# A second mixture of experts: sums read from PSUM, operands in another order, raw pieces and stored operands moved

## The chip, the cores and the metric

The kernel runs on one core of a Trainium2 chip. The metric is device time in microseconds of one execution; before the change the median of three runs is 2117.43 us (2113.62 to 2118.29). Engine names are those of the profile: PE is TensorE's matmul, PEld its weight load, DVE VectorE, ACT ScalarE, POOL GpSimd, SP SyncE, which here only issues DMAs.

## The reference

Three layers run one after the other over 2304 tokens of width 512: retention attention, a first mixture, and the second mixture, which this change is about:

```python
def _moe2_ref(x, w_gate, w1, w2):          # N=2304, D=512, E=8 experts, F=1024
    logits = x @ w_gate
    P = np.exp(logits - logits.max())
    for _ in range(8):                      # row and column sums in turn
        P /= P.sum(1, keepdims=True) + 1e-09
        P /= P.sum(0, keepdims=True) + 1e-09
        P *= N / E
    out = 0
    for e in range(E):
        out += P[:, e:e+1] * (np.maximum(x @ w1[e], 0.0) @ w2[e])
```

All of it is fp32. The kernel keeps that precision on PE by splitting each operand into a high half (rounded to fp32r) and a low half (operand minus high half), and multiplying three pairs: high by high, high by low, low by high.

## The kernel before, in words

The second mixture cuts the hidden width into 32 units of 256 (8 experts x 4) and the tokens into 3 passes of 768, so there are 96 steps, `s` from 0 to 95; `q = s // 32` is the pass and `u = s % 32` the unit. Both matrix products of a unit are done as a 2 x 2 block scheme with seven products in place of eight: seven token operands (`X1K`, `T2`, ...) times seven weight operands of w1 (`AK`, `S2`, `S1`, `AL`, `S3`, `S4`, `BL`), each of six matmuls of 384 columns (`product`, L933). Their sums are formed with adds on DVE out of three kinds of PSUM bank, `x`, `y` and `z`: `p1` copies the first product, `u2`, `p5` and `u3` (L1118 to L1146) are partial sums in SBUF.

In pass 0 (L1069) a step also makes the operands that the later passes reload. `weight_tasks` (L618) is a list of small closures for the next unit: ACT rounds the high halves (`hi`), POOL subtracts (`lo`, L686, and the sums of w1 pieces, L662), and SP writes the finished parts to DRAM. `mixed_tasks` (L577) does the same for the four mixed operands of w2: four sums on DVE in one closure (L590), high halves on ACT (L596), low halves on POOL (L600), eight writes. The list is worked off by `slot(k)` and between the six `mm2` (L951), which multiply the activations of the step before by w2, plainly, and add into `acc` on DVE (L976, L985). Four PSUM banks `m` hold mm2's results, and PE stops when DVE has not emptied the oldest. The relu is split as well: ACT takes the high half (L943), DVE the low one (L947). The last product of a step (`BL`) and its relu are put off into the next step (`late_product`). In steps 0 to 4 the row and column sums of the gate run on DVE between products (`tick`). From step 4 on, `tasks` holds DVE and ACT work that forms the token operands of the next pass; five of these pieces (`late`) have to wait for the last step of a pass.

In passes 1 and 2 (L1312) a step has seven places `k`. Place k runs `first_(s, k)`, the k-th product of this step with its adds and the fold of relu and gate weight (L1171), then `after`, which splits activation operands for the second product (ACT high half L1182, POOL low half L1183, POOL differences L1186), and then `second_(s-1, k)`, one block of nine matmuls (L1268) of the step before, whose result DVE adds into `acc` (L1281), through two double banks `p`. Which operand the block of place k reads is in `ORDER_S`; the blocks E7, E5, E6 and E4 read differences of activations (D3, D1, D2, D4), E3 reads B22. Behind each use SP reloads that weight operand for the next step, 256 KB at a time. `finish` (L1288) forms a pass's output from the seven sums once the pass is over.

Every engine works in the order in which the program issues to it: a closure's place in a list is its place in the queue of each engine that it uses, SP's DMAs included. No scheduler moves anything (`manual_schedule`).

## Time and profile before

| | |
|---|---|
| runs | 2117.43 us median (2113.62 to 2118.29) |
| profiled execution | 2117.14 us, its span 2115.3 us |
| mean granted TensorE clock | 0.975 of full |
| busy | PE 1993.8 us (94%), DVE 1556.8 (74%), POOL 1441.1 (68%), ACT 675.8 (32%) |
| pass 0 | about 501 to 1111 us, passes 1 and 2 from there to the end |

The span runs from the first to the last instruction; the profiled execution's time has 1.8 us more around it. Busy time of PE is a modelled figure, since matmuls overlap, so a step is better judged by when the next one starts. Steps are cut where ACT copies the first product of a step: line L1106 in pass 0 (32 of them, from 501.3 to 1073.5 us) and L1196 in the later passes (64, from 1111.4 to 2081.5 us).

### The profile page before, as it was taken

How to read it: one execution, taken by the hardware profiler on the slowest of the kernel's cores; microseconds unless marked ns; L12 is line 12 of the kernel's file. 1: busy time of each engine (PE TensorE's matmuls, PEld its weight loads, DVE VectorE, ACT ScalarE, POOL GpSimd, SP SyncE). 2: the span in 40 equal slices, each digit the busy share in tenths (PEclk: the TensorE clock that was granted, in tenths of full speed). 3: DMA queues.
4: the chain of work that ended last, by engine and by line, in shares of the span. 5: the costliest groups of instructions: out<-in, count | busy, mean ns of one | idle time of the engine just before them, and what ended most of it. 6: DMA issues, size and time to landing. Idle time of an engine off the chain costs nothing.

```text
span 2115.3 us, 35267 instructions
## 1 busy us (share of the span) xinstructions
PE 1993.8 (94%) x12369; PEld 1818.9 (86%) x12369; DVE 1556.8 (74%) x2318; ACT 675.8 (32%) x1408; POOL 1441.1 (68%) x1393
## 2 busy tenths in 40 slices
PE   7899999999888998999959999999998999999998
PEld 6688888877777887888859999999997999999997
DVE  7865877535877787887855787877776777777777
ACT  3334223334344343333423322222223322222221
POOL 4654555534576677777736788887877878787875
PEclk9999999999999899999989999999999999999999
DMA  8411111014667777777768888788786888788873
GB/s 314 161 40 36 55 37 44 26 55 144 205 234 249 250 253 251 251 277 278 268 196 245 261 251 249 251 249 253 239 252 206 273 252 249 248 238 262 250 252 119
DMA packets 269584, 434.74 MB, mean 206 GB/s; under 512 B 25936, under 2 KB 119008, under 8 KB 269152
## 3 DMA queue, kind: packets, MB, share of 16 engines
q1 hardware_dynamic: 269264, 432.47, 63.3%
q8 instruction: 99, 1.62, 0.3%
q14 instruction: 77, 0.63, 0.1%
q10 hardware_dynamic: 144, 0.02, 0.0%
HBM read 310.15 MB, written 122.23 MB: 204 GB/s over the span
## 4 chain that ended last, share of the span: by engine, by line
POOL 24%; DVE 20%; PE 15%; issue 6%; ACT 4%; DMA 1%; SPq 1%; POOLq 0%; DVEq 0%; ACTq 0%
POOL wo L1183 11%; POOL u L1186 5%; PE ps_m L963 5%; DVE mix L590 4%; DVE u L1171 4%; PE ps_y L933 4%; PE ps_p L1268 3%; POOL p L1186 3%; POOL r L1186 2%; POOL p L1345 2%; DVE acc L1281 2%; PE ps_z L933 2%; PE ps_x L933 2%; DVE wo L947 1%; ACT wo L1182 1%
## 5 line engine op out<-in xcount | busy, mean ns | idle before, releaser
L1268 PE MATMUL ps_p<-wi,wo 128*128 128x256 f32 x3969 | 550.0, 283 | 15.7 <-ACT acc L1279 5.4
L1268 PEld LDWEIGHTS ps_p<-wi,wo 128*128 128x128 f32 x3969 | 522.5, 189 | 36.0 <-ACT p L1196 22.5
L1281 DVE TENSOR_TENSOR acc<-ps_p,acc 128x768 f32<-128x768 f32 x427 | 400.2, 950 | 99.9 <-PE ps_p L1268 92.1
L963 PE MATMUL ps_m<-wo,wo 128*128 128x512 f32 x1152 | 296.9, 413 | 67.4 <-DVE acc L985 58.8
L933 PE MATMUL ps_y<-xh,wi 128*128 128x384 f32 x1152 | 342.6, 342 | 1.0 <-DVE u L1201 1.0
L963 PEld LDWEIGHTS ps_m<-wo,wo 128*128 128x128 f32 x1152 | 224.6, 198 | 126.9 <-DVE acc L985 70.9
L1183 POOL TENSOR_TENSOR wo<-u,wo 128x384 fp32r<-128x384 f32 x191 | 195.0, 1021 | 163.0 <-ACT wo L1182 160.6
L1182 ACT ACTIVATE wo<-u 128x384 fp32r<-128x384 f32 x191 | 100.4, 526 | 490.7 <-POOL u L1186 286.8
L933 PE MATMUL ps_z<-xh,wi 128*128 128x384 f32 x768 | 231.9, 343 | 2.4 <-DVE u L1151 2.4
L933 PE MATMUL ps_x<-xh,wi 128*128 128x384 f32 x768 | 227.6, 337 | 0.0
L933 PEld LDWEIGHTS ps_y<-xh,wi 128*128 128x128 f32 x1152 | 218.7, 194 | 3.3 <-DVE u L1201 1.2
L442 POOL TENSOR_TENSOR gl<-sg,gh 128x512 fp32r<-128x512 f32 (+1 forms) x80 | 95.6, 1195 | 173.1 <-ACT gh L441 134.9
L933 PE MATMUL ps_y<-xl,wi 128*128 128x384 f32 x576 | 196.8, 342 | 0.0
L430 PE MATMUL ps<-xh,wi 128*128 128x512 f32 (+1 forms) x640 | 186.4, 370 | 0.0
L455 PE MATMUL ps<-gh,wo 128*128 128x512 f32 (+1 forms) x640 | 184.2, 368 | 0.3
L686 POOL TENSOR_TENSOR wi<-r,wi 128x512 fp32r<-128x512 f32 x64 | 71.0, 1109 | 147.3 <-ACT wi L679 129.4
L933 PEld LDWEIGHTS ps_z<-xh,wi 128*128 128x128 f32 x768 | 145.7, 193 | 6.6 <-DVE u L1151 6.5
L1183 POOL TENSOR_TENSOR wo<-p,wo 128x384 fp32r<-128x384 f32 x127 | 148.1, 1166 | 2.2 <-ACT wo L1182 1.9
L933 PEld LDWEIGHTS ps_x<-xh,wi 128*128 128x128 f32 x768 | 142.4, 189 | 0.0
L440 DVE TENSOR_TENSOR sg<-ps,sg 128x512 f32<-128x512 f32 (+1 forms) x80 | 51.0, 637 | 120.6 <-ACT sg L439 118.5
L430 PEld LDWEIGHTS ps<-xh,wi 128*128 128x128 f32 x640 | 116.4, 188 | 23.5 <-issue 3.4
L455 PEld LDWEIGHTS ps<-gh,wo 128*128 128x128 f32 x640 | 116.2, 189 | 20.9 <-POOL wo L166 1.1
(151 smaller groups left out, 3844.4 us busy)
## 6 DMA issues: line engine op xcount, KB each, us to landing
wi<-first SPq DMA_DIRECT2D x448, 256.0 KB, 3.3
wi<-second SPq DMA_DIRECT2D x441, 256.0 KB, 3.2
first<-wi SPq DMA_DIRECT2D x90, 512.0 KB, 2.7
r<-in_w_dram SPq DMA_DIRECT2D x65, 512.0 KB, 4.7
second<-wo SPq DMA_DIRECT2D x96, 256.0 KB, 2.2
second<-wi SPq DMA_DIRECT2D x128, 128.0 KB, 1.9
second<-mix SPq DMA_DIRECT2D x128, 128.0 KB, 1.9
aux<-in_vk_dram SPq DMA_DIRECT2D x16, 544.0 KB, 6.1
```

Of the source, the lines that this page charges most:

```text
L430: nc.tensor.matmul(out=t[:, 0:n], lhsT=a[:, d, fs], rhs=x[:, d, t0 : t0 + n], start=d == 0 and a is wh and x is xh, stop=d == KD - 1 and a ...
L442: nc.gpsimd.tensor_tensor(out=gl[:, f, 0:n], in0=gf[:, 0:n], in1=r32(gh[:, f, 0:n]), op=ALU.subtract)
L455: nc.tensor.matmul(out=po[d][:, 0:n], lhsT=a[:, f, ds_], rhs=x[:, f, 0:n], start=f == 0 and a is wh and x is gh, stop=f == KF - 1 and a is wl,
L590: nc.vector.tensor_tensor(out=out, in0=a, in1=b, op=op)
L933: nc.tensor.matmul(out=t[:, 0:N], lhsT=w[:, o, hw, c], rhs=xq(q, x, hx, c), start=begin and c == 0 and i == 0, stop=end and c == 1 and i == 2,
L963: nc.tensor.matmul(out=t, lhsT=x[:, is_], rhs=w[:, h, f], start=f == 0 and k == 0, stop=f == 1 and k == 2,)
L1171: nc.vector.scalar_tensor_tensor(out=to, in0=c, scalar=0.0, in1=pr_of(s)[:, t * N : (t + 1) * N], op0=ALU.max, op1=ALU.mult,)
L1182: nc.scalar.activation(out=h, in_=src, func=ACTF.Copy)
L1183: nc.gpsimd.tensor_tensor(out=l, in0=src, in1=r32(h), op=ALU.subtract)
L1186: nc.gpsimd.tensor_tensor(out=to, in0=a, in1=b, op=ALU.subtract)
L1268: nc.tensor.matmul(out=t[:, j * QF : (j + 1) * QF], lhsT=x[:, js], rhs=w[:, o, hw], start=k == 0, stop=k == 2,)
L1281: nc.vector.tensor_tensor(out=e, in0=t[:, 0 : 3 * QF], in1=e, op=ALU.add)
```

## The change

In pass 0 the four mixed sums become four closures with a fifth, `begin`, ahead of them, in which ACT copies the left half of the raw w2 piece into the `y` bank that the step does not use; three of the sums read it there. They are placed between the tasks of w1 and those of w2 and one after the other between the mm2. The second add for `u3` goes: `p5` is now `z + p1` on DVE, and the three finished sums are written into the PSUM banks `x`, `z` and `y` themselves, from where relu reads both halves. `y` is two fixed banks, `x` gets two and `m` three. The raw w2 piece is loaded by `load_next` one step ahead, behind POOL's last read of the one before; the mixed operands of unit 0 are made in step 0 and no longer in step 31. Token tasks run one per step behind the fourth mm2. The stored operands of w2 are laid out so that two share one DMA.

In passes 1 and 2 the order of the blocks is E1, E3, E7, E5, E6, E2, E4: B22 comes second, and D3, D1 and D2 one place later. `p5` is formed by DVE out of PSUM, no longer by ACT and POOL, and the sums stay in PSUM until the fold. Weights come in five DMAs for the first product and four for the second. `after` stands ahead of the block. `finish` is on DVE alone and hands out one sum per step (two in the second step of a pass), and the late token tasks one per place.

```diff
     def mixed_tasks(s, raw):
-        def sums():
-            r = raw().rearrange("p b (j d) -> p b j d", j=2)
-            t = box["t"] = raw2[1].tile([P, 2, 2, QF], F32, tag="mix", name="mix")
-            for out, a, b, op in (
-                (t[:, 1, 1], r[:, 0, 1], r[:, 1, 1], ALU.add),
-                (t[:, 0, 1], r[:, 0, 0], r[:, 0, 1], ALU.subtract),
-                (t[:, 0, 0], t[:, 1, 1], r[:, 0, 0], ALU.subtract),
-                (t[:, 1, 0], r[:, 1, 0], t[:, 0, 0], ALU.subtract),
-            ):
+        def begin():
+            box["p"] = ys[(s + 1) % 2].rearrange("p (b d) -> p b d", b=2)
+            box["t"] = raw2[1].tile([P, 2, 2, QF], F32, tag="mix", name="mix")
+            nc.scalar.activation(out=box["p"], in_=raw()[:, :, 0:QF], func=ACTF.Copy)
+
+        def sums(i):
+            def go():
+                r = raw().rearrange("p b (j d) -> p b j d", j=2)
+                p, t = box["p"], box["t"]
+                out, a, b, op = (
+                    (t[:, 1, 0], p[:, 0], r[:, 0, 1], ALU.subtract),
+                    (t[:, 1, 1], r[:, 0, 1], r[:, 1, 1], ALU.add),
+                    (t[:, 0, 0], t[:, 1, 1], p[:, 0], ALU.subtract),
+                    (t[:, 0, 1], p[:, 1], t[:, 0, 0], ALU.subtract),
+                )[i]
                 nc.vector.tensor_tensor(out=out, in0=a, in1=b, op=op)
 
...
             def put():
-                for b in range(2):
-                    o = ((E6, E3), (E7, E5))[j][b]
-                    nc.sync.dma_start(out=w2st(s)[:, o, 0], in_=r32(w[:, b]))
-                    nc.sync.dma_start(out=w2st(s)[:, o, 1], in_=box["t"][:, b, j])
-
-            return [go, low, put]
-
-        return [sums] + high(1) + high(0)
+                d = part(second_store[s], (3, 1)[j], 2)
+                nc.sync.dma_start(out=d[:, 0], in_=r32(w))
+                nc.sync.dma_start(out=d[:, 1], in_=box["t"][:, j])
+
+            return [high, low, put]
+
+        return [begin] + [sums(i) for i in range(4)], rest(1) + rest(0)
 
+    def load_next(s):
+        e, u = divmod(s, NQ)
+        ahead2[s] = raw2[0].tile([P, 2, DM], F32, tag="r2", name="r2")
+        src = w2[e, u * QF : (u + 1) * QF, :].rearrange("(f p) d -> p f d", p=P)
+        nc.sync.dma_start(out=ahead2[s], in_=src)
...
-        second_ = [hi("w"), lo("w", slice(0, 1)), mixed[0], lo("w", slice(1, 2))]
-        second_ += [lambda: keep_plain(s - 1)] + mixed[1:]
+
+        def following():
+            if s < NU:
+                load_next(s)
+
+        mix = mixed[0]
+        second_ = [hi("w"), lo("w", slice(0, 1)), lo("w", slice(1, 2))]
+        second_ += [lambda: keep_plain(s - 1), following] + mixed[1]
         if s == NU:
-            return [load] + second_
-        ts = [load, sums(S1), hi("a"), sums(S3), hi("b"), hi(S1), lo("a", al), put(AK, 2)]
-        ts += [lo(S1, al), put(S1, 2), sums(S2), sums(S4), hi(S2), lo("b", al), put(BL, 1)]
-        return ts + [lo(S2, al), put(S2, 2)] + second_
+            return [load, mix[0]] + second_[:1] + mix[1:] + second_[1:]
+        ts = [load, sums(S1), hi("a"), mix[0], sums(S3), hi("b"), hi(S1), lo("a", al)]
+        ts += [put(AK, 2), lo(S1, al), put(S1, 2), sums(S2), sums(S4), hi(S2), lo("b", al)]
+        ts += [put(BL, 1), lo(S2, al), put(S2, 2), mix[1], second_[0], mix[2], second_[1]]
+        ts += [second_[2], mix[3], second_[3], mix[4]]
+        return ts + second_[4:]
...
+    for s in range(2):
+        keep_first(s, 0, 7)
...
-    psum = {tag: open_banks(tag, n) for tag, n in (("x", 1), ("y", 2), ("z", 1), ("m", 4))}
+    ys = []
+    psum = {tag: open_banks(tag, n) for tag, n in (("y", 2), ("z", 1), ("x", 2), ("m", 3))}
...
-    ORDER_S = ((E1, B11), (E7, D3), (E5, D1), (E6, D2), (E3, B22), (E2, B21), (E4, D4))
+    ORDER_S = ((E1, B11), (E3, B22), (E7, D3), (E5, D1), (E6, D2), (E2, B21), (E4, D4))
...
-        wt = weight_tasks(s + 1) if s else []
+        wt = weight_tasks(s + 1) if s else begun[2]
         if s == 0:
-            keep_first(0, 0, 7)
-        if s == 1:
-            keep_first(1, 0, 7)
-            keep_plain(0)
-        if s == NU - 1:
-            box = {}
-
-            def again():
-                box["r"] = raw2[0].tile([P, 2, DM], F32, tag="r2", name="r2")
-                nc.sync.dma_start(
-                    out=box["r"], in_=w2[0, 0:QF, :].rearrange("(f p) d -> p f d", p=P)
-                )
-
-            wt += [again] + mixed_tasks(0, lambda: box["r"])
+            load_first(2)
...
-            if tasks and k % 6 == 2 and s % 2:
-                tasks.pop(0)()
-            if xt and k >= 1:
-                xt.pop(0)()
+            if s == NU - 1 and k in (2, 5, 9):
+                drop_late()
...
-            for o in ORDER_F:
-                load_first_ops(NU, o)
+            for o, n in ((AK, 2), (S2, 2), (S1, 2), (BL, 1)):
+                load_first_ops(NU, o, n)
...
-        y = bank2("y")
+        y = ys[s % 2]
...
-        nc.scalar.activation(out=p5, in_=z[:, 0:N], func=ACTF.Copy)
+        nc.vector.tensor_tensor(out=p5, in0=z[:, 0:N], in1=p1, op=ALU.add)
...
-        for i in (3, 4, 5, 0, 1, 2) if s else ():
-            while i != 3 and len(wt) > 5:
+        for n, i in enumerate((3, 4, 5, 0, 1, 2) if s else ()):
+            mm2(s - 1, i)
+            for _ in range(-(-len(wt) // (6 - n))):
                 wt.pop(0)()
-            mm2(s - 1, i)
-            if wt:
-                wt.pop(0)()
+            if tasks and n == 3:
+                tasks.pop(0)()
             tick()
...
-        u3 = tmp("u3")
-        nc.vector.tensor_tensor(out=u3, in0=y[:, 0:N], in1=p1, op=ALU.add)
-        nc.vector.tensor_tensor(out=u3, in0=u3, in1=p5, op=ALU.add)
-        relu_high(s, 1, 1, u3)
-        relu_low(s, 1, 1, u3)
+        c = x[:, 0:N]
+        nc.vector.tensor_tensor(out=c, in0=y[:, 0:N], in1=p5, op=ALU.add)
+        relu_high(s, 1, 1, c)
+        relu_low(s, 1, 1, c)
         product(s, z, S4, X2L, False, True)
         tick()
-        nc.vector.tensor_tensor(out=u2, in0=z[:, 0:N], in1=u2, op=ALU.add)
-        relu_high(s, 0, 1, u2)
-        relu_low(s, 0, 1, u2)
-        while xt:
-            xt.pop(0)()
+        c = z[:, 0:N]
+        nc.vector.tensor_tensor(out=c, in0=c, in1=u2, op=ALU.add)
+        relu_high(s, 0, 1, c)
+        relu_low(s, 0, 1, c)
 
         def rest(s=s, y=y, p1=p1):
             product(s, y, BL, T4, False, True)
             tick()
-            nc.vector.tensor_tensor(out=p1, in0=y[:, 0:N], in1=p1, op=ALU.add)
-            relu_high(s, 1, 0, p1)
-            relu_low(s, 1, 0, p1)
+            c = y[:, 0:N]
+            nc.vector.tensor_tensor(out=c, in0=c, in1=p1, op=ALU.add)
+            relu_high(s, 1, 0, c)
+            relu_low(s, 1, 0, c)
...
+            load_first_ops(s + 1, S2, 1)
...
-            nc.scalar.activation(out=d["p5"], in_=d["z"][:, 0:N], func=ACTF.Copy)
+            nc.vector.tensor_tensor(out=d["p5"], in0=d["z"][:, 0:N], in1=d["p1"], op=ALU.add)
...
+            load_first_ops(s + 1, AK, 2)
...
         if k == 4:
             product(s, d["y"], S3, T3, False, False)
+            load_first_ops(s + 1, S1, 2)
+            c = d["x"][:, 0:N]
+            nc.vector.tensor_tensor(out=c, in0=d["y"][:, 0:N], in1=d["p5"], op=ALU.add)
             d["u3"] = tmp("u3")
-            nc.vector.tensor_tensor(out=d["u3"], in0=d["y"][:, 0:N], in1=d["p5"], op=ALU.add)
-            folded(s, d["u3"], 1, d["u3"])
+            folded(s, c, 1, d["u3"])
         if k == 5:
             product(s, d["z"], S4, X2L, False, True)
-            nc.vector.tensor_tensor(out=d["u2"], in0=d["z"][:, 0:N], in1=d["u2"], op=ALU.add)
-            folded(s, d["u2"], 1, d["u2"])
+            load_first_ops(s + 1, S4, 1)
+            c = d["z"][:, 0:N]
+            nc.vector.tensor_tensor(out=c, in0=c, in1=d["u2"], op=ALU.add)
+            folded(s, c, 1, d["u2"])
...
-            nc.vector.tensor_tensor(out=d["p1"], in0=d["y"][:, 0:N], in1=d["p1"], op=ALU.add)
-            folded(s, d["p1"], 0, d["p1"])
-        load_first_ops(s + 1, ORDER_F[k])
+            load_first_ops(s + 1, BL, 1)
+            c = d["y"][:, 0:N]
+            nc.vector.tensor_tensor(out=c, in0=c, in1=d["p1"], op=ALU.add)
+            folded(s, c, 0, d["p1"])
...
+        if i in (0, 3, 4, 6):
+            load_second_ops(s + 1, lead, n)
...
-            op(g, E2, E1, E2, ALU.add, (0, 0)),
...
-        fin = finish(q - 1) if u == 1 and q > 1 else []
+        if u == 1 and q > 1:
+            fin += finish(q - 1)
...
-            for o, _ in ORDER_S:
-                load_second_ops(s, o)
+            for lead, n in ((0, 1), (3, 2), (1, 2), (5, 2)):
+                load_second_ops(s, lead, n)
+            drop_late()
...
-            if k == 2:
-                d = steps[s]
-                nc.gpsimd.tensor_tensor(out=d["p5"], in0=d["p5"], in1=d["p1"], op=ALU.add)
             if tasks and k == 1:
                 tasks.pop(0)()
-            if u == NU - 1 and k > 1 and late:
-                assert not tasks
-                late.pop(0)()
-                if late:
-                    late.pop(0)()
-            second_(s - 1, k)
+            if u == NU - 1 and k in (2, 5) or u == 0 and k in (0, 2, 3):
+                drop_late()
+            if u == 0 and k == 4:
+                assert not late
             if k in (4, 6):
                 after(s, k)
-            for _ in range(2):
-                if fin:
-                    fin.pop(0)()
+            second_(s - 1, k)
+            if fin and (k in (1, 2) if u == 1 else k == 1):
+                fin.pop(0)()
```

In passes 1 and 2 `load_first_ops(s, o, n)` and `load_second_ops(s, lead, n)` are one DMA each over n neighbouring operands. `next_tokens` and `drop_late` hand out the token tasks as before, in the places that the text above names.

## Rows read from the trace of the kernel before

**Rows 1.** Busy time by stretch: start:end, length, each engine's us (instructions), granted clock, DMA.

```profile
core 0: us, PE busy (x) PEld busy (x) DVE busy (x) ACT busy (x) POOL busy (x), PEclk, DMA share, GB/s
501.26:509.13 7.87, 7.87 (x45) 7.47 (x44) 3.50 (x7) 2.43 (x6) 0.00 (x0) 1.00 0.99 341
509.13:619.83 110.70, 93.60 (x412) 80.66 (x411) 84.36 (x164) 43.38 (x83) 66.21 (x62) 0.89 0.65 224
619.83:865.17 245.34, 222.69 (x1022) 194.96 (x1021) 192.84 (x261) 92.34 (x179) 174.22 (x156) 0.93 0.71 248
865.17:1073.52 208.35, 194.84 (x940) 170.53 (x939) 165.70 (x230) 82.00 (x160) 157.87 (x142) 0.98 0.78 270
1073.52:1111.42 37.90, 17.50 (x76) 15.01 (x75) 17.49 (x27) 7.71 (x17) 8.28 (x6) 0.73 0.57 169
1144.73:1569.45 424.72, 421.45 (x2947) 412.96 (x2946) 335.67 (x438) 122.23 (x263) 341.70 (x337) 1.00 0.82 250
1584.59:1642.36 57.77, 48.98 (x312) 46.30 (x311) 39.57 (x48) 19.28 (x39) 42.07 (x39) 0.94 0.69 208
```

**Rows 2.** Timeline, two places of a step of pass 1: start, us, engine, line, out<-in.

```profile
1506.42 0.34 PE L933 MATMUL ps_x<-xh,wi 128*128 128x384 f32 x1
...
1507.47 1.23 PE L1268 MATMUL ps_p<-wi,wo 128*128 128x256 f32 x9
...
1508.42 1.33 POOL L1183 TENSOR_TENSOR wo<-p,wo 128x384 fp32r<-128x384 f32 x1
...
1508.53 0.34 PE L933 MATMUL ps_y<-xh,wi 128*128 128x384 f32 x1
...
1509.84 1.31 PE L1268 MATMUL ps_p<-wi,wo 128*128 128x256 f32 x9
```

**Rows 3.** Chain that ended last, one mm2 stretch of pass 0: start, us, what.

```profile
736.97 8.36 PE ps_m L963 x36
```

**Rows 4.** Waits of PE over the span: us in total, times, longest.

```profile
PE ps_m L963 <- DVE acc L985: 58.8, 24, 20.4
```

**Rows 5.** Timeline of a step of pass 0; in brackets idle before and its releaser.

```profile
720.13 1.53 DVE L590 TENSOR_TENSOR mix<-r 128x256 f32<-128x256 f32 x2
...
724.41 2.71 DVE L985 SCALAR_TENSOR_TENSOR acc<-ps_m,pr,acc 128x512 f32<-128x512 f32 x4
725.21 2.93 PE L963 MATMUL ps_m<-wo,wo 128*128 128x512 f32 x6 [2.97 <-DVE acc L985]
```

**Rows 6.** Timeline of step 31, the last of pass 0.

```profile
1078.33 0.54 SPq L644 DMA_DIRECT2D r<-in_w_dram  x1
...
1086.65 1.06 ACT L679 ACTIVATE wo<-r 128x1024 fp32r<-128x1024 f32 x1 [11.42 <-DMA r<-in_w_dram]
...
1099.27 0.76 DVE L590 TENSOR_TENSOR mix<-r 128x256 f32<-128x256 f32 x2 [4.85 <-DMA r<-in_w_dram]
...
1101.55 5.47 PE L963 MATMUL ps_m<-wo,wo 128*128 128x512 f32 x12 [20.40 <-DVE acc L985]
```

**Rows 7.** Groups by line and form, 700 to 1075 us: busy, mean ns | idle before.

```profile
L600 POOL TENSOR_TENSOR mix<-mix,wi 128x512 fp32r<-128x512 f32 x42 | 54.0, 1306 | 0.8 <-issue 0.8
...
L590 DVE TENSOR_TENSOR mix<-r 128x256 f32<-128x256 f32 x42 | 38.6, 958 | 0.7 <-DMA r<-in_w_dram 0.7
...
L1146 DVE TENSOR_TENSOR u<-u,p 128x384 f32<-128x384 f32 x21 | 21.4, 1020 | 0.7
...
L1145 DVE TENSOR_TENSOR u<-ps_y,p 128x384 f32<-128x384 f32 x21 | 11.7, 557 | 8.9 <-PE ps_y L933 8.9
```

**Rows 8.** DMA issues by line: times, KB each, median us from issue to landing.

```profile
r<-in_w_dram SPq DMA_DIRECT2D x65, 512.0 KB, 4.7
```

**Rows 9.** Groups by line and form, 1140 to 1570 us: busy, mean ns | idle before.

```profile
L1281 DVE TENSOR_TENSOR acc<-ps_p,acc 128x768 f32<-128x768 f32 x196 | 183.2, 949 | 40.9 <-PE ps_p L1268 37.0 <-ACT p L1196 1.9
```

**Rows 10.** Timeline of step 65, the second of pass 2.

```profile
1628.39 5.51 DVE L1295 TENSOR_TENSOR acc<-acc 128x768 f32<-128x768 f32 x4
...
1635.74 2.15 PE L1268 MATMUL ps_p<-wi,wo 128*128 128x256 f32 x9 [3.19 <-ACT acc L1279]
```

**Rows 11.** Timeline of the end: the sums of the last `finish` on DVE.

```profile
2099.61 6.33 DVE L1295 TENSOR_TENSOR acc<-acc 128x768 f32<-128x768 f32 x5 [2.66 <-POOL acc L1295]
```

More of the change, by code (lines that the diff above doesn't have):

```diff
@@ L616, in retention_moe_kernel, with load_first @@
     ahead = {}
+    ahead2 = {}
+    def load_next(s):
[3 more added lines that the diff above has]
+        nc.sync.dma_start(out=ahead2[s], in_=src)
+    def load_first(s):
+        e, u = divmod(s, NQ)
+        pool = raw2[1] if s > 0 and s % 2 == 0 else raw2[0]
+        ahead[s] = pool.tile([P, KD, QF], F32, tag="r1", name="r1")
+        src = w1[e, :, u * QF : (u + 1) * QF].rearrange("(k p) f -> p k f", p=P)
+        nc.sync.dma_start(out=ahead[s], in_=src)
     def weight_tasks(s, apart=False):
@@ L622, in weight_tasks @@
         w, w2t = wq(s), w2q(s - 1)
-        def place(s):
-            e, u = divmod(s % NU, NQ)
-            return e, slice(u * QF, (u + 1) * QF)
-        def load_first(s):
-            e, fs = place(s)
-            pool = raw2[1] if s > 0 and s % 2 == 0 else raw2[0]
-            ahead[s] = pool.tile([P, KD, QF], F32, tag="r1", name="r1")
-            src = w1[e, :, fs].rearrange("(k p) f -> p k f", p=P)
-            nc.sync.dma_start(out=ahead[s], in_=src)
         def load():
@@ L639, in load @@
                 box["r1"] = ahead.pop(s)
+            if s == 1:
+                load_next(0)
             if s:
-                e, fs = place(s - 1)
-                box["r2"] = raw2[0].tile([P, 2, DM], F32, tag="r2", name="r2")
-                src = w2[e, fs, :].rearrange("(f p) d -> p f d", p=P)
-                nc.sync.dma_start(out=box["r2"], in_=src)
+                box["r2"] = ahead2.pop(s - 1)
             if 1 < s < NU - 1:
@@ L696, in weight_tasks @@
             late = [hi("a"), hi(S1), lo("a", al), hi("b"), lo(S1, al), sums(S2), sums(S4)]
-            return early, late + [hi(S2), lo("b", al), lo(S2, al)]
+            mixed = mixed_tasks(0, lambda: box["r2"])
+            after = [lambda: keep_plain(0)] + mixed[0] + [lambda: load_next(1)] + mixed[1]
+            return early, late + [hi(S2), lo("b", al), lo(S2, al)], after
         def put(o, n):
@@ L1055, in tick @@
         ticks[0] += 1
+    ys += [bank2("y") for _ in range(2)]
     sink = sinkhorn_steps()
@@ L1064, in token_step, with drop_late @@
         if q + 1 < NPASS and u == 4:
[L1065 to L1067 removed]
+            now, then = next_tokens(q + 1)
+            tasks.extend(now)
+            late.extend(then)
+    def drop_late():
+        if late:
+            assert not tasks
+            late.pop(0)()
     for s in range(NU):
[L1070 removed]
+        wt = weight_tasks(s + 1) if s else begun[2]
         if s == 0:
[L1072 to L1085 removed]
+            load_first(2)
         if s == PR_STEP:
[L1087 removed]
+            wt = pr_tasks() + wt
         token_step(s)
[L1089 to L1091 removed]
         def slot(k):
@@ L1263, in second_ @@
         h, l = operand(b)
-        w = w2s()
+        lead, n, x = W2PART[o]
+        w = part(wi[1], lead, n)[:, :, x]
         for j in range(3):
             js = slice(j * P, (j + 1) * P)
-            for k, (x, hw) in enumerate(((h, 0), (h, 1), (l, 0))):
+            for k, (a, hw) in enumerate(((h, 0), (h, 1), (l, 0))):
                 nc.tensor.matmul(
                     out=t[:, j * QF : (j + 1) * QF],
-                    lhsT=x[:, js],
-                    rhs=w[:, o, hw],
+                    lhsT=a[:, js],
+                    rhs=w[:, hw],
                     start=k == 0,
@@ L1302, in finish @@
         return [
-            op(g, E2, E1, E2, ALU.add, (0, 0)),
+            op(v, E2, E1, E2, ALU.add, (0, 0)),
             op(v, E1, E1, E6, ALU.add),
```

87 lines of the change are left out of this document (41 added, 46 removed).

## The prediction

> **What bounds the kernel now.** Read first the busy time by stretches, cut where the steps begin [rows 1]: what counts is the mean step and how much of it PE works. One step of pass 0 has seven products of six matmuls and six mm2 of six; one of passes 1 and 2 has seven products and seven second-mixture blocks of nine. What PE needs without a wait is read from places where it has none: a product 1.05 us (1506.42 to 1507.47) and a block 1.06 (to 1508.53) [rows 2], 36 mm2 matmuls 8.36 [rows 3]. So the floor is 7 x 1.05 + 8.36 = 15.7 us for a step of pass 0, and 7 x 2.11 = 14.8 for one of passes 1 and 2. Against it [rows 1]: steps 1 to 5 take 110.7 (22.1 each), 6 to 18 245.3 (18.9), 19 to 30 208.4 (17.4), step 31 37.9, 28 steps of pass 1 in one stretch 424.7 (15.17), the three around the change of pass 57.8 (19.3). Pass 0 holds over 100 us above its floor, passes 1 and 2 some 35. The largest wait of PE is for DVE's accumulation L985, 58.8 us in 24 waits, 20.4 in one [rows 4].
>
> Then the timeline of one step shows why. After the first L985, DVE has four L590 sums in a row (from 720.13), and only at 724.41 the next four accumulations; PE, out of banks, stands 2.97 us before its last mm2 [rows 5]. The mean granted clock is 0.93 in steps 6 to 18 and 0.98 in 19 to 30 [rows 1] (full is 2.4 GHz, the lower level 1.2): part of what such a wait costs comes after it. At step 31 the same place costs 20.4: the raw w2 load is issued at 1078.33 behind seven operand loads, a second one (`again`) follows, DVE's last sums start only at 1099.27, and PE's fifth mm2 waits until 1101.55 [rows 6]. In passes 1 and 2 one block per step starts late: the y product at 1508.53 should end at 1509.58, the E7 block starts at 1509.84, just after POOL's low half of D3 (1508.42 + 1.33 = 1509.75) [rows 2]; that 0.26, and its weight loads, is most of 15.17 - 14.77.
>
> **The change, part by part.**
>
> *Sums spread out (pass 0).* The four sums no longer stand together behind accumulation one: one or two each go behind accumulations one to three. Three of them read `p` from PSUM in place of a second SBUF operand; ACT's `begin` puts it there. The price of such a sum: the short end is 0.4 (the pair at 1099.27, where POOL rests, takes 0.76 [rows 6]), the long one 0.96, the mean in pass 0 [rows 7]. L1145, with one operand in PSUM, takes 0.56 for 384 columns, against 1.02 for L1146 with both in SBUF [rows 7], so I take 0.4 for three and 0.96 for the fourth. DVE then has per mm2 (1.39 of PE) an accumulation of 0.7 (724.41, four in 2.71 [rows 5]) and a sum, 1.7 at most, and a bank comes back before PE asks for it, though mm2 has three banks and no longer four. The wait of rows 5 goes; late next is the ring of three banks, with some 2 us in hand.
>
> *Adds after S3 and S4 (pass 0).* The second add L1146 goes (1.02 mean), the relu's low half reads PSUM (0.56, as L1145). p5 becomes a DVE add of 0.56 where ACT had a copy. One new wait comes: z is now overwritten in place, so the next step's S1 product must wait for the low half of relu on z, no longer only for the add. With S3's end at 0: add 0.2 to 0.8, ACT high half to 1.3, low half to 1.9, z add to 2.5, high half to 3.1, low half to 3.7; PE runs S4, AK, BL, S2 and is at S1 at 4 x 1.05 = 4.2. Half a us in hand. Queued behind it on PE is everything; a token task of two DVE operations (9 of steps 4 to 18), now placed late in mm2, costs 2.0 if each takes what L1146 does, and DVE then comes about 0.9 late to S3's add. I add 0.7 per step to steps 6 to 18; nothing and 1.3 are the ends.
>
> *x with two banks, y fixed.* `begin` writes the y bank of the step before; on ACT it waits for the late relu and for the raw w2 piece, and behind it stand the high halves of w1 and relu of x, which PE needs only a step later. POOL: 12 operations, 13.2 us per step [rows 1], still under 15.7.
>
> *Raw w2 loaded a step ahead.* The load moves from the start of a task list to behind POOL's last read of the old piece, in SP's queue behind `keep_plain`, ahead of the four (formerly eight) puts. SP issues about 12 DMAs per step, before 17. It takes 4.7 us to land [rows 8], and `begin` asks for it about 5 later. Writes and reads stay as they are: 270 GB/s at 17.4 us a step [rows 1], 4.7 MB, becomes 300 at 15.7, under the 341 that step 0 shows. `again` and its sums move to step 0, where PE has nothing of them to wait for: +0.6.
>
> Pass 0 by steps: 1 to 5 still carry the row and column sums of the gate on DVE: from 22.1 to 19.5, -13. Steps 6 to 18: 13 x 16.4 against 245.3, -32. 19 to 30: 12 x 15.8 against 208.4, -19. Step 31: no load in it, three late token tasks on DVE before mm2 (some 2 us of wait): 18 against 37.9, -20. With step 0, -83. From below: 1 to 5 at 17, the rest at the floor, -109. From above: -39, rival one's case with steps 1 to 5 unchanged.
>
> *D3 and D1 one place later, B22 second (passes 1, 2).* Needed at place 2 and no longer 1, D3 has 2.1 us more; the p5 add leaves POOL too (about 1.0 of 12.2 per step [rows 1]). B22 is ready a step ahead. Of what is moved past: the first loads now go in five DMAs and the second in four (before seven and seven) per step, AK three places later, still four places (8.4 us) ahead of use. DVE at places 4 to 6 has 0.95 + 2 x 0.56 = 2.07 of 2.11; full (0.95 is L1281 [rows 9]), but places 0 to 3 give back. 60 steps from 15.17 to 14.8: -22; bounds 0 and -23.
>
> *Change of pass.* Sums of `finish` all on DVE, one per step and no longer two per place; late token tasks one per place. PE's wait of 3.19 for ACT's copy [rows 10] came from DVE, which from 1628.39 had four of them (L1295, 5.51) in front of the product's fold that ACT needed first. 57.8 for three steps becomes 47.5: -10; bounds -13 and -3.
>
> *End.* Seven sums on DVE without POOL, which stood 2.66 us in front of five of 6.33 [rows 11]: -2, bounds +1 and -4. *Transition step 32:* ACT's copies still wait behind POOL: 0.
>
> Sum: -83 - 22 - 10 - 2 = -117, against the profiled execution's 2117.1 (span 2115.3 and 1.8 around it; the median of the runs is 2117.4): 2000.
>
> Two rules of the Trainium skill bear on this. VectorE: DVE Perf Modes (Rules for kernel authors) speaks against the edit: it says to copy a matmul's output to SBUF first if many operations follow, and this change does the contrary. L1145 reads PSUM in 0.56, L1146 takes 1.02 from SBUF [rows 7]: the trace disagrees, at least while POOL works beside it; by the rule the operations that stay in PSUM would be the dearer ones, about what rival four gives. SBUF (SBUF: two separate sides) states that DVE with two SBUF inputs and GpSimd take turns on a port pair, one blocking the other; by that POOL would gain what DVE gains, which lowers rival one's chance.
>
> **Rivals.** One: POOL becomes the bound of pass 0 (13.2 busy, and it waits for ACT's high halves, now behind `begin`): steps 6 to 30 at 17.4, the mean that steps 19 to 30 have now. For it: POOL has the smallest reserve. Against: its idle of 4 us a step is waiting, not work. Then pass 0 gives 13 + 19 + 20 = 52 with no gain in 19 to 30: 2031.
>
> Two: another operand takes D3's place, since DVE is full at places 4 to 6: passes 1, 2 stay at 15.16: 2022.
>
> Three: pass 0 meets its floor nearly everywhere, -109 in place of -83, and the change of pass too, -13: 1971.
>
> Four: operations that write PSUM (no row has one on DVE) take 1.0 like L1146. Two of them delay z's low half by 0.9, less the 0.5 in hand, and the third slows the late relu: about 0.9 in each of 31 steps: 2028.
>
> Five, the other side: a loop through the single w2 buffer. `begin` cannot start before the piece lands; the load cannot start before POOL's last read, about 10.6 later (13.2 less the mix's two low halves of 1.31 [rows 7]). A step is then at least 10.6 plus the landing time. At 4.7 that is 15.3, under the floor. At step 31 a load took 8.3 behind seven others (1078.33 to ACT's start at 1086.65) [rows 6]: 18.9. To lose the whole gain of the other parts (step 31 20, passes 34) and be slower, 30 steps must pass 20.6, a landing of over 10: nothing in pass 0 shows that. At 11 a step is 21.6: 30 x (21.6 - 18.8) = +84, less 54: 2147.
>
> **How the numbers follow.** Forecast 0.45, rival one 0.2, two 0.1, three 0.13, four 0.06, five 0.04; 0.02 that errors cancel. The range 1964 to 2048 reaches from below three to just short of one and two together (2053); left out are five, errors, and the far ends of the others, under 0.2 in all. The measurement tells 0.2% (4.2 us) from no change: faster 0.94, same 0.02, slower 0.04; only five, and cancelling errors, are not faster.
>
> **What would show it.** Right: PE's waits for L985 near none; the step of 19 to 30 at 15.7 to 16; step 31 under 20; places of 2.11 without a gap in passes 1 and 2, step 14.8; `finish` steps under 17. Wrong: ACT's `begin` waiting for a DMA, POOL busy without gaps in pass 0, PE waiting at S1 for the low half of z in each step, or one block of each step still starting 0.3 late. Above 2060 the pass-0 part has failed as a whole.

## The result, and the profile after

The changed kernel takes 2002.03 us (median of 4 runs, 2001.21 to 2004.29), the kernel before 2117.24 beside it: ratio 0.946, 95% interval 0.9444 to 0.9477. The forecast was 2000. The profiled execution after took 2001.21 us, with a span of 1999.1.

First the busy time by stretches, cut at the same steps as before: step 0, steps 1 to 5, 6 to 18, 19 to 30, 31, 28 steps of pass 1, the three at the change of pass (columns as in [rows 1]).

```profile
501.91:509.27 7.36, 7.36 (x42) 6.96 (x41) 4.87 (x11) 3.39 (x8) 2.67 (x3) 1.00 1.00 337
509.27:612.12 102.85, 88.01 (x412) 76.41 (x412) 75.36 (x164) 44.53 (x83) 65.15 (x62) 0.95 0.69 249
612.12:821.58 209.46, 206.27 (x1021) 183.14 (x1019) 163.17 (x263) 92.77 (x179) 168.82 (x156) 1.00 0.81 289
821.58:1008.00 186.42, 185.96 (x935) 168.00 (x934) 129.93 (x228) 83.58 (x160) 149.63 (x142) 1.00 0.84 301
1008.00:1030.61 22.61, 18.38 (x80) 15.88 (x79) 13.14 (x21) 6.72 (x14) 5.35 (x4) 0.85 0.77 277
1063.82:1479.54 415.72, 415.72 (x2942) 413.71 (x2941) 338.61 (x466) 117.84 (x235) 311.62 (x309) 1.00 0.77 255
1494.34:1539.15 44.81, 44.75 (x319) 44.43 (x317) 33.44 (x47) 18.45 (x36) 34.82 (x34) 1.00 0.79 264
```

Against [rows 1]: PE is busy all of steps 19 to 30 and of pass 1, at full clock (1.00). What is left above a floor of 15.5 us per step stands in steps 1 to 5 (25 us), in steps 6 to 18 (8) and in step 31 (7). PE's largest waits for DVE in this part of the program (pass 0 of the second mixture), against 58.8 for one line in [rows 4] (total, times, longest):

```profile
PE ps_m L988 <- DVE acc L1010: 6.3, 2, 4.2
PE ps_z L958 <- DVE wo L972: 6.2, 11, 1.9
PE ps_m L988 <- DVE acc L1001: 5.8, 5, 2.5
...
PE ps_m L988 <- DVE sm_col L845: 3.1, 1, 3.1
```

Line L1010 is the accumulation that was L985. The step that answers to [rows 5], on DVE: accumulations and sums alternate, and DVE waits for PE before the last two.

```profile
841.61 0.75 DVE L1010 SCALAR_TENSOR_TENSOR acc<-ps_m,pr,acc 128x512 f32<-128x512 f32 x1 [0.31 <-PE ps_m L988]
842.28 0.42 DVE L594 TENSOR_TENSOR mix<-ps_y,r 128x256 f32<-128x256 f32 x1
842.99 0.75 DVE L1010 SCALAR_TENSOR_TENSOR acc<-ps_m,pr,acc 128x512 f32<-128x512 f32 x1 [0.29 <-PE ps_m L988]
843.65 0.86 DVE L594 TENSOR_TENSOR mix<-r 128x256 f32<-128x256 f32 x1
...
847.07 0.75 DVE L1010 SCALAR_TENSOR_TENSOR acc<-ps_m,pr,acc 128x512 f32<-128x512 f32 x1 [0.45 <-PE ps_m L988]
848.43 0.75 DVE L1010 SCALAR_TENSOR_TENSOR acc<-ps_m,pr,acc 128x512 f32<-128x512 f32 x1 [0.61 <-PE ps_m L988]
```

Durations by form in steps 19 to 30, for [rows 7]: an add that writes PSUM, and the sums with p in PSUM and without.

```profile
L594 DVE TENSOR_TENSOR mix<-r 128x256 f32<-128x256 f32 x12 | 9.9, 824 | 0.0
L1157 DVE TENSOR_TENSOR ps_x<-ps_y,p 128x384 f32<-128x384 f32 x12 | 6.8, 567 | 3.7 <-PE ps_y L958 3.7
...
L594 DVE TENSOR_TENSOR mix<-ps_y,r 128x256 f32<-128x256 f32 x12 | 5.0, 417 | 0.5 <-DMA second<-mix 0.5
```

Step 31, for [rows 6]: on DVE the first sum waits for the mix tile, whose write to DRAM is issued at 1007.62 and takes 6.1, with the operand loads issued from 1008.71 under way beside it; the other sums and a token task of 2.90 follow, and only then the accumulations. PE waits 4.23 instead of 20.4.

```profile
1013.85 0.43 DVE L594 TENSOR_TENSOR mix<-ps_y,r 128x256 f32<-128x256 f32 x1 [3.04 <-DMA second<-mix]
...
1016.24 2.90 DVE L767 TENSOR_TENSOR xl<-acc,xh 128x384 fp32r<-128x384 f32 x2
1019.06 2.06 DVE L1010 SCALAR_TENSOR_TENSOR acc<-ps_m,pr,acc 128x512 f32<-128x512 f32 x3
```

```profile
1019.86 6.96 PE L988 MATMUL ps_m<-wo,wo 128*128 128x512 f32 x18 [4.23 <-DVE acc L1010]
```

At the end, for [rows 11], seven sums stand in one piece on DVE, with no wait for POOL:

```profile
1982.62 7.46 DVE L1315 TENSOR_TENSOR acc<-acc 128x768 f32<-128x768 f32 x7
```

### The profile page after: what moved, and what is told of

It is laid out like the page before. It is cut to its first block, busy times and chain, and to the rows that moved or that the text cites. A ratio compares the mean times of both kernels' runs of the same rounds, so it can differ in the third digit from the quotient of the medians.

```text
span 1999.1 us, 34461 instructions
## 1 busy us (share of the span) xinstructions
PE 1945.5 (97%) x12369; PEld 1800.6 (90%) x12369; DVE 1479.5 (74%) x2386; ACT 667.8 (33%) x1344; POOL 1347.0 (67%) x1325
## 4 chain that ended last, share of the span: by engine, by line
PE 63%; DVE 5%; ACT 1%; DMA 1%; issue 0%; POOL 0%; SPq 0%; DVEq 0%; ACTq 0%; POOLq 0%
PE ps_p L1287 23%; PE ps_y L958 13%; PE ps_m L988 9%; PE ps_z L958 9%; PE ps_x L958 9%; DVE acc L1010 1%; DVE xl L767 1%; DVE mix L594 1%; DVE t L748 1%; DVE wo L972 0%; ACT wo L968 0%; DVE acc L1315 0%; DMA second<-mix 0%; PE ps_m L1392 0%; DVE ps_x L1157 0%
## 5 line engine op out<-in xcount | busy, mean ns | idle before, releaser
L1287 PE MATMUL ps_p<-wi,wo 128*128 128x256 f32 x3969 | 543.6, 281 | 1.8 <-ACT acc L1299 1.7
L1301 DVE TENSOR_TENSOR acc<-ps_p,acc 128x768 f32<-128x768 f32 x427 | 407.3, 954 | 133.8 <-PE ps_p L1287 133.6
L958 PE MATMUL ps_y<-xh,wi 128*128 128x384 f32 x1152 | 337.1, 337 | 1.3 <-DVE ps_x L1157 1.3
L988 PE MATMUL ps_m<-wo,wo 128*128 128x512 f32 x1152 | 276.2, 397 | 15.2 <-DVE acc L1010 6.3
L988 PEld LDWEIGHTS ps_m<-wo,wo 128*128 128x128 f32 x1152 | 219.3, 192 | 62.8 <-DVE acc L1001 7.6
L958 PEld LDWEIGHTS ps_y<-xh,wi 128*128 128x128 f32 x1152 | 212.7, 188 | 5.4 <-DVE ps_x L1157 3.7
L1194 POOL TENSOR_TENSOR wo<-r,wo 128x384 fp32r<-128x384 f32 x127 | 129.0, 1016 | 48.5 <-ACT wo L1193 40.8
L1010 DVE SCALAR_TENSOR_TENSOR acc<-ps_m,pr,acc 128x512 f32<-128x512 f32 x168 | 124.4, 746 | 44.0 <-PE ps_m L988 39.2
L455 PEld LDWEIGHTS ps<-gh,wo 128*128 128x128 f32 x640 | 116.2, 189 | 21.0 <-POOL wo L166 1.1
```

Source lines behind the costliest of these rows:

```text
L455: nc.tensor.matmul(out=po[d][:, 0:n], lhsT=a[:, f, ds_], rhs=x[:, f, 0:n], start=f == 0 and a is wh and x is gh, stop=f == KF - 1 and a is wl,
L958: nc.tensor.matmul(out=t[:, 0:N], lhsT=w[:, o, hw, c], rhs=xq(q, x, hx, c), start=begin and c == 0 and i == 0, stop=end and c == 1 and i == 2,
L988: nc.tensor.matmul(out=t, lhsT=x[:, is_], rhs=w[:, h, f], start=f == 0 and k == 0, stop=f == 1 and k == 2,)
L1010: nc.vector.scalar_tensor_tensor(out=oa, in0=tv, scalar=pr[:, ti, e : e + 1], in1=oa, op0=ALU.mult, op1=ALU.add)
L1194: nc.gpsimd.tensor_tensor(out=l, in0=src, in1=r32(h), op=ALU.subtract)
L1287: nc.tensor.matmul(out=t[:, j * QF : (j + 1) * QF], lhsT=a[:, js], rhs=w[:, hw], start=k == 0, stop=k == 2,)
```

## The experiments

Theory: the terms of the prediction. Each run but the last undoes one or two of them in the changed kernel; the token tasks' new place and the joined loads are undone in none. The times, with the stretches of the profiled executions (us):

```
kernel          median   steps 1-5   6-18     19-30    31      63-65   above the changed kernel
changed         2002.0   102.9       209.5    186.4    22.6    44.8
block_psum      2002.9   109.0       204.1    186.5    21.5    44.8     +0.9
spread_sbuf     2013.5   103.8       218.2    187.7    22.6    44.8    +11.5
block_sbuf      2034.6   116.9       216.2    200.4    21.3    44.8    +32.6
relu_sbuf       2010.8   105.7       213.4    186.8    22.3    45.3     +8.8
r2_late_sbuf    2028.9   103.9       220.3    189.5    31.6    44.8    +26.9
r2_late         2075.8   100.1       239.5    219.5    32.4    44.8    +73.8
x1m4            2040.5   105.5       231.4    199.8    18.4    45.4    +38.5
order_old2      2003.0   102.5       209.5    186.5    22.6    45.2     +1.0
p5_pool         2004.2   102.9       209.5    186.4    22.6    45.6     +2.2
turn_old        2014.6   102.5       209.5    186.4    22.6    52.9    +12.6
best            1985.4    97.5       201.8    186.4    15.5    44.8    -16.6
```

Against the kernel before, the intervals of the ratio reach at most 0.0025 to either side (0.9369 to 0.9407 for best).

**The four sums: their place, or their length.** block_psum puts them in one block again, spread_sbuf lets them read the raw piece, block_sbuf does both.

```diff
-        ts += [put(BL, 1), lo(S2, al), put(S2, 2), mix[1], second_[0], mix[2], second_[1]]
-        ts += [second_[2], mix[3], second_[3], mix[4]]
+        ts += [put(BL, 1), lo(S2, al), put(S2, 2), four]     # four: mix[1] to mix[4]
+        ts += second_[:4]
```
```diff
-            box["p"] = ys[(s + 1) % 2].rearrange("p (b d) -> p b d", b=2)
-            nc.scalar.activation(out=box["p"], in_=raw()[:, :, 0:QF], func=ACTF.Copy)
+            box["p"] = raw()[:, :, 0:QF]
```

> The changed kernel, with the four sums of a piece in one block again, behind the first accumulation of mm2; three of them still read p from PSUM. Theory: with these three at 0.42 and the fourth at 0.89 the block is 2.1 us, accumulation two ends some 4.9 after mm2 began, and PE wants that bank only after four mm2 of 1.39 (5.6): no wait, 2000 to 2008, so the place of the sums is worth nothing once they are short. Rival: the block itself was the wait, whatever a sum takes; then PE waits 2 to 3 us per step in steps 2 to 30 again, 2060 to 2090.

> The changed kernel without ACT's copy of p into PSUM: the four sums stay spread out and read the raw piece in SBUF. Theory: a sum takes 0.9 in place of 0.42, 1.4 us more of DVE per step; per mm2 of 1.39 an accumulation of 0.7 and a sum still fit for the most part, so steps 20 to 30 stay at 15.5 to 15.8 and steps with a token task gain 0.5 to 1.5: 2005 to 2018. Rival: reading from PSUM is what paid; then each step of pass 0 is 1.4 longer, 2040 or more.

> The changed kernel with both undone: four sums in one block behind the first accumulation, all from the raw piece in SBUF. Theory: the block is 3.7, accumulation two ends at 6.5 where PE wants the bank at 5.6, so PE waits 1 us or a little more per step and DVE comes late to the adds behind mm2: 1 to 2.5 us per step of 2 to 30, 2030 to 2070. If block_psum and spread_sbuf both cost little and this much, either edit alone would have taken the wait away. Rival: neither edit matters and the earlier load is the gain: under 2015.

Undone alone they cost 0.9 and 11.5, together 32.6: the block fits the ring of the three banks of mm2 once its sums are short, and long sums mostly fit once they are apart. With both undone PE waits again in nearly every step (steps 1 to 31):

```profile
PE ps_m L991 <- DVE acc L1013: 23.3, 28, 3.8
```

In steps 6 to 18 the short block is even 5.4 faster than the spread sums, in 1 to 5 it is 6.2 slower. In spread_sbuf the sums take 0.74 to 1.35 (steps 19 to 30), hidden there, and not in steps with a token task.

```profile
L593 DVE TENSOR_TENSOR mix<-r 128x256 f32<-128x256 f32 x24 | 17.6, 738 | 3.2 <-DMA second<-mix 2.1 <-POOL s L669 1.1
L593 DVE TENSOR_TENSOR mix<-r,mix 128x256 f32<-128x256 f32 x12 | 16.3, 1354 | 0.4
```

**Activations of pass 0 in SBUF again.** u3 by two adds, p5 by a copy, relu from SBUF:

```diff
...
-        c = x[:, 0:N]
-        nc.vector.tensor_tensor(out=c, in0=y[:, 0:N], in1=p5, op=ALU.add)
+        c = tmp("u3")
+        nc.vector.tensor_tensor(out=c, in0=y[:, 0:N], in1=p1, op=ALU.add)
+        nc.vector.tensor_tensor(out=c, in0=c, in1=p5, op=ALU.add)
...
```

> The changed kernel with the activations of pass 0 (not of passes 1 and 2) kept in SBUF again: p5 a copy on ACT, u3 by two adds, the relu halves read from SBUF. Theory: DVE works 1.0 for the second add and some 0.4 for each of three low halves more, less 0.55 for p5, about 1.7 per step; it has room for it (12 of 15.5 busy in steps 20 to 30), and the wait at S1 for the low half of z goes: 2000 to 2012. Rival: these edits carry the gain of steps 6 to 30, and the time rises by 1 us or more per step: 2030 or more.

+8.8, within what was expected. Of the 9.3 by which the profiled execution is longer, 6.7 stand in steps 1 to 18 and 2.4 ahead of step 1; steps 19 to 30, without token tasks, hide it. The wait at S1 does not go, as the expectation had it. In steps 6 to 18 it stands behind each token task of two DVE operations, as in the changed kernel, only that it is now for the add:

```profile
PE ps_z L958 <- DVE u L1164: 6.9, 10, 1.2
```

**The raw w2 load.** In r2_late it stands at the start of its step's list again; r2_late_sbuf also takes ACT's copy of p away.

```diff
-            if s == 1:
-                load_next(0)
             if s:
+                load_next(s - 1)
                 box["r2"] = ahead2.pop(s - 1)
...
```

> The changed kernel, with the raw w2 piece of a step loaded at the start of that step's list again, in step 31 behind the operand loads of pass 1; the single load of each piece stays. Theory: the load ahead of time pays in step 31 above all: about 8 us there (a load behind seven others took 8.3), and up to 1 us in each other step of pass 0, because ACT's copy into PSUM now waits for the piece with other ACT work queued behind it: 2010 to 2040. Rival: the load was hidden anyway, and the cost of step 31 in the kernel before was its second load and its sums alone: 2000 to 2005.

> The load of raw w2 at the start of its step's list again, and no copy of p into PSUM: the sums, spread out, read the raw piece. Theory: in r2_late the dear thing was ACT's copy that waits for the piece with ACT's other work behind it; without it nothing wants the piece before mm2, some 7 us after the issue, and only step 31 pays, about 10 above the same kernel with the load ahead (2013): 2018 to 2030. Rival: the late load itself costs 2 to 3 us in each step of pass 0: 2060 to 2085.

Alone the late load costs 15.4 over spread_sbuf, 9 of them in step 31. With the copy it costs 73.8, about twice the upper end of what was expected: ACT waits 4.3 on average for the piece (103.6 over 24, steps 6 to 30). Behind the copy in ACT's queue stands the high half of relu, DVE's low half waits for that, and DVE's accumulations stand behind the low half; PE waits for them again. The waits of ACT, one step in which ACT and DVE show it, and the waits of PE:

```profile
ACT ps_y L582 <- DMA r<-in_w_dram: 103.6, 24, 5.9
...
876.40 0.60 ACT L582 ACTIVATE ps_y<-r 128x512 f32<-128x512 f32 x1 [5.69 <-DMA r<-in_w_dram]
...
877.75 0.56 DVE L970 SCALAR_TENSOR_TENSOR wo<-ps_x,wo 128x384 fp32r<-128x384 f32 x1 [6.03 <-ACT wo L966]
...
PE ps_m L986 <- DVE acc L1008: 57.4, 23, 14.8
```

So the load ahead is what makes the copy into PSUM affordable. The first half of rival five's mechanism, ACT's copy held by the piece's landing, exists; that the load then waits for POOL's last read, which would close the loop, is not shown. In the changed kernel the load is early enough.

**Banks.** One x bank and four for mm2: `("x", 1), ("m", 4)` for `("x", 2), ("m", 3)`.

> The changed kernel with one x bank and four banks for mm2, as before, in place of two and three. Theory: the next step's AK product must now wait for the low half of relu on x, which ends about 1.75 after S3 while S4 ends after 1.04: 0.7 of wait in each of 31 steps, +22, 2018 to 2030, and no gain from the fourth bank. Rival: the bank is free in time or the fourth one gives as much back: 1998 to 2005.

+38.5, above the expected 2018 to 2030; the one large wait behind it, in steps 0 to 31:

```profile
PE ps_x L958 <- DVE wo L972: 46.5, 32, 4.4
```

The wait comes as the theory says, 0.79 in a step of 19 to 30, but such a step is 1.12 longer (199.84 - 186.42, over 12):

```profile
945.15 0.34 PE L958 MATMUL ps_z<-xh,wi 128*128 128x384 f32 x1
946.28 0.44 PE L958 MATMUL ps_x<-xh,wi 128*128 128x384 f32 x1 [0.79 <-DVE wo L972]
946.56 0.34 PE L958 MATMUL ps_x<-xl,wi 128*128 128x384 f32 x1
```

Matmuls of a product otherwise start about 0.17 apart, before the one ahead has ended. Here the first start comes 1.13 after the last one and the second 0.28 after the first, whose weight load starts only with it: 1.07 more in all. In steps with a token task it costs more. Step 31 is 4.2 shorter than in the changed kernel, so the fourth bank, from which nothing was expected, is worth something there; what either half of the edit does alone was not run.

**D3's place and the p5 add.** In order_old (2257.1 us) the split of B22 stands ahead of the block that reads it, so that this block used and waited for the next step's operand; it says nothing on the question. order_old2 moves the split behind it; p5_pool gives the add back to POOL.

```diff
-    ORDER_S = ((E1, B11), (E3, B22), (E7, D3), (E5, D1), (E6, D2), (E2, B21), (E4, D4))
+    ORDER_S = ((E1, B11), (E7, D3), (E5, D1), (E6, D2), (E3, B22), (E2, B21), (E4, D4))
```
```diff
-            nc.vector.tensor_tensor(out=d["p5"], in0=d["z"][:, 0:N], in1=d["p1"], op=ALU.add)
+            nc.scalar.activation(out=d["p5"], in_=d["z"][:, 0:N], func=ACTF.Copy)
+            nc.gpsimd.tensor_tensor(out=d["p5"], in0=d["p5"], in1=d["p1"], op=ALU.add)
```

> The changed kernel, with D3, D1 and D2 back at places 1 to 3 of the second mixture and B22 back at place 4; all else stays (the p5 add on DVE, the joined loads). Theory: the place was the wait, so each of the 60 steps of passes 1 and 2 goes from 14.79 back to about 15.13, +20 us, 2022, and PE waits again ahead of the E7 block for POOL's low half of D3. Rival: the gain came from the add that left POOL, or from the joined loads; then the step stays at 14.79 and the time at 2002.

> The changed kernel, with D3, D1 and D2 at places 1 to 3 and B22 at place 4, and the splits behind places 4 and 6 issued after that place's block again, so that B22 is overwritten only when its block has read it; p5 stays on DVE, the joined loads stay. Theory: each of the 60 steps of passes 1 and 2 goes from 14.79 to about 15.1 with PE late at the E7 block: 2018 to 2024. Rival: the p5 add that left POOL or the joined loads made the gain, and the step stays at 14.79: 2000 to 2005.

> The changed kernel, with p5 of passes 1 and 2 again as a copy on ACT and an add on POOL in place of one add on DVE. Theory: with D3 at place 2 POOL has a whole place (2.1 us) in hand, so one more operation of about 1.0 per step is hidden: 14.79 per step, 2002 (2000 to 2005). Rival: POOL's load was the cause, and the step goes to 15.0 or more: 2015 to 2022.

order_old2 loses nothing: the theory falls. Its trace shows D3's low half (POOL, 1451.42) done at 1452.45, 1.9 before the E7 block at place 1 starts (the second PE row, 1454.38); before, it ended 0.17 after that block should have started [rows 2].

```profile
1451.42 1.03 POOL L1194 TENSOR_TENSOR wo<-p,wo 128x384 fp32r<-128x384 f32 x1
...
1452.27 1.23 PE L1287 MATMUL ps_p<-wi,wo 128*128 128x256 f32 x9
...
1454.38 1.23 PE L1287 MATMUL ps_p<-wi,wo 128*128 128x256 f32 x9
```

In the kernel before, the low half was not even what held the block, though the prediction and the expectations read it so. The first two of the block's matmuls read the high half, and the first was already late: at 1509.84 for 1509.58. It writes the PSUM bank that DVE's accumulation of the block before last has to empty, and that ends at the same moment as the low half (1508.79 + 0.95 = 1509.74, against 1509.75). PE's queue held a wait for DVE's semaphore for 2.39, from 1507.39 to 1509.78, and the block's first weight load follows at 1509.81, although the view names another releaser:

```profile
1508.79 1.81 DVE L1281 TENSOR_TENSOR acc<-ps_p,acc 128x768 f32<-128x768 f32 x2
...
L1268 PEldq EVENT_SEMAPHORE  x1: 2392/2392/2392, 1507.4 to 1507.4; - x1
...
1509.81 1.14 PEld L1268 LDWEIGHTS ps_p<-wi,wo 128*128 128x128 f32 x9 [0.39 <-ACT p L1196]
```

By the trace's semaphore marks that weight load comes 60 or 61 ns after DVE's in 53 of the 56 steps, and 47 to 59 ns after POOL's. So the step was lost to DVE being late with an accumulation.

What made DVE late is seen in the idle time of its add after S3. First the kernel before, 28 steps of pass 1, then order_old2 and p5_pool, the same steps (busy, mean ns, idle before it):

```profile
L1215 DVE TENSOR_TENSOR u<-ps_y,p 128x384 f32<-128x384 f32 x28 | 15.6, 558 | 44.6 <-POOL p L1345 43.5 <-PE ps_p L1268 1.1
```

```profile
L1229 DVE TENSOR_TENSOR ps_x<-ps_y,p 128x384 f32<-128x384 f32 x28 | 15.7, 560 | 1.6
...
L1230 DVE TENSOR_TENSOR ps_x<-ps_y,p 128x384 f32<-128x384 f32 x28 | 15.9, 567 | 4.0
```

In the kernel before, DVE stood 1.55 per step for POOL's p5 add, which came behind the splits of B21 and D4 in POOL's queue. The folds and accumulations came late by that, as did POOL's difference of the folds and D3. In p5_pool the add is on POOL again but two operations earlier, ahead of D4's difference and split; there the same add of DVE shows 4.0 of idle in 28 steps and none for POOL. The folds of DVE are also shorter, by 1.06 per step (two of 0.77 and one of 1.19 before, 0.56 each now):

```profile
L1171 DVE SCALAR_TENSOR_TENSOR u<-u,r 128x384 f32<-128x384 f32 x56 | 43.3, 773 | 1.9
L1171 DVE SCALAR_TENSOR_TENSOR p<-p,r 128x384 f32<-128x384 f32 x28 | 33.2, 1185 | 1.0
```

Either is more than the 0.26 that the block was late. No run has the folds in SBUF again, or the p5 add in its old place in POOL's queue, so which of the two was needed is open. The joined loads were not undone either; before, no wait of PE in passes 1 and 2 is put down to a DMA.

**The change of pass.** Late token tasks and the sums of `finish` two per place again, the first and last of these on POOL.

```diff
-            if u == NU - 1 and k in (2, 5) or u == 0 and k in (0, 2, 3):
-                drop_late()
+            if u == NU - 1 and k > 1:
+                drop_late()
+                drop_late()
...
-            if fin and (k in (1, 2) if u == 1 else k == 1):
-                fin.pop(0)()
+            for _ in range(2):
+                if fin:
+                    fin.pop(0)()
```

> The changed kernel, with the change of pass as before: late token tasks two per place from place 2 of the last step of a pass, the sums of finish two per place, the first and the last of them on POOL again, at the end of the program too. Theory: the three steps 63 to 65 go from 44.8 back to 55 to 58 us and the end grows by some 2.8: 2013 to 2018. Rival: the boundary gained from the other edits (p5 and D3), and these steps stay under 48: 2002 to 2006.

+12.6 as expected, but spread over four steps: 63 to 66 take 71.3 against 59.5. The end grows by 1.8, for the 2.8 expected.

**What is left.** best cuts DVE's bursts in the stretches that are still above the floor. Step 31 takes its piece up at the places of the other steps; the task of the gate's row and column sums is cut in two; a token task is done in halves.

```diff
-            return [load, mix[0]] + second_[:1] + mix[1:] + second_[1:]
+            ts = [load] + 2 * idle + [mix[0]] + 14 * idle + [mix[1], second_[0], mix[2]]
+            return ts + second_[1:3] + [mix[3], second_[3], mix[4]] + second_[4:]
...
-        return [highest, turned, overall, spread, exps] + [sums, both] * 7 + [sums, cols]
+        start = [highest, turned, overall, spread, exps, idle, idle]
+        return start + [sums, cols, rows] * 7 + [sums, cols]     # at ticks 0, 1, 3 of six
...
+        half = tasks.pop(0) if tasks else None                   # ahead of mm2
+        if half:
+            half((0,))
...
-            if tasks and n == 3:
-                tasks.pop(0)()
+            if half and n == 2:
+                half((1,))
```

> The changed kernel with three edits in stretches of their own: step 31 takes up the w2 piece at the same places as other steps (sums behind mm2, no longer in front of them); the long DVE task of the gate's normalization in steps 1 to 5 is cut in two; a token task of steps 4 to 18 is done one half ahead of mm2 and one behind its third. Theory: what waits are left come from DVE bursts of 3 us and more: step 31 from 22.6 to 17 or 18, steps 1 to 5 from 102.9 to 95 to 99, steps 6 to 18 from 209.5 to 203 to 206: 1982 to 1994. Rival: DVE's total in these stretches is the bound, not where its bursts stand: 1998 to 2004.

1985.4, the fastest. Each of the three stretches gains; steps 6 to 18 and step 31 are now at 15.5 each, with PE busy throughout:

```profile
512.70:610.15 97.45, 84.74 (x403) 71.61 (x403) 74.67 (x162) 42.22 (x81) 63.83 (x60) 0.98 0.70 250
610.15:811.92 201.77, 201.58 (x1014) 182.45 (x1013) 149.78 (x263) 92.65 (x178) 166.74 (x154) 1.00 0.85 299
...
998.34:1013.85 15.51, 15.51 (x80) 14.06 (x79) 11.19 (x21) 6.74 (x15) 5.36 (x4) 1.00 0.88 324
```

## Why the prediction was right, and where its steps were not

The terms, from the two profiled executions (spans 2115.3 and 1999.1, -116.2):

```
term                    forecast   measured
steps 1 to 5             -13        -7.9   (110.70 to 102.85)
steps 6 to 18            -32       -35.9   (245.34 to 209.46)
steps 19 to 30           -19       -21.9   (208.35 to 186.42)
step 31                  -20       -15.3   (37.90 to 22.61)
step 0                    +0.6      -0.5
passes 1, 2              -22       -19.5  (28 steps of pass 1 424.7 to 415.7, of pass 2 424.0 to 414.2,
                                          steps 62 and 66 30.2 to 29.5)
change of pass           -10       -13.0   (57.77 to 44.81)
end                       -2        -2.8
```

These add up to -116.8; 0.6 is lost again ahead of step 0. That the sum comes within 2 us of the forecast is partly luck: the terms miss by 0.8 to 5.1 each, 24 in all, and the misses cancel to 0.6.

- *Floor.* 15.7 was 0.2 too high: mm2's 8.36 [rows 3] holds the tail of its last matmul, and the next product starts after 8.20. Steps take 15.51.
- *Sums spread out.* Price nearly right (0.42 and 0.82 to 0.89 for 0.4 and 0.96), cause half right: block_psum shows that in steps 6 to 30 the place was worth nothing once the sums were short. Both undone give back 20.8 of the 57.8 that these steps gained.
- *Adds after S3 and S4.* An add that writes PSUM takes 0.57, so rival four falls; relu_sbuf, which keeps these sums in SBUF, is 8.8 slower. The Trainium skill (VectorE: DVE Perf Modes, section Rules for kernel authors) leaves two ways for work on a matmul's output: accept the PSUM source, or copy to SBUF first if many operations follow. The prediction named the second alone; by relu_sbuf it is the first that pays here. The wait at S1 came in steps 6 to 18 only with token tasks, 3.2 in 7 waits, a third of what was charged, and z being overwritten in place is not its reason: relu_sbuf, which takes that away, has it too.
- *x with two banks.* The step given no price. It is what carries the add in place: with one bank, and a fourth for mm2, +38.5. The ring of three banks for mm2 held, as said.
- *Raw w2 a step ahead.* Charged as a matter of step 31 alone. It is worth 15.4, and 73.8 as the condition of ACT's copy.
- *Step 31.* 22.6 and not 18: the first sum's 3.04 for the mix tile wasn't foreseen, and it put the sums and a token task in front of the accumulations. best, which moves the sums in between the accumulations, has 15.5.
- *Steps 1 to 5.* Gained 5 less than forecast; what remains is partly the long task of the gate's sums, since cutting it gives 5.4.
- *D3 one place later.* The size was nearly right by luck, the step wrong: by order_old2 the move is worth nothing beside the rest. The prediction took the block's wait to be for POOL's low half of D3, which ends 0.01 after the accumulation of DVE that the block waited for, and so did not come to DVE's 1.55 for POOL's p5 add and to its long folds, though it mentions that the add leaves POOL.
- *What no run undoes.* Taken one by one, the edits undone (both on the sums, the activations in SBUF, the late load without the copy) give back 12.8 of the 35.9 in steps 6 to 18 and 16.2 of the 21.9 in steps 19 to 30. Whether the rest is their joint effect or, in steps 6 to 18, also that of the token tasks' new place is open.
- *Rivals.* One: POOL works 12.5 of 15.5 in steps 19 to 30 and bounds nothing. Two: pass 1 has no wait left. Three: steps 19 to 30 did reach the floor, 6 to 18 and 31 do so in best, 1 to 5 in neither.
